# A decode layer on one core: PV in four column tiles, one loop over all batches, and w3 and w4 laid out in long runs

## The chip, the core and the metric

The kernel runs on one core of a Trainium2 chip. A core has five engines that run their own instruction streams and meet at semaphores: TensorE (PE, matrix products, with weight loads shown apart as PEld), VectorE (DVE), ScalarE (ACT), GpSimd (POOL) and SyncE (SP). Sixteen DMA engines bring data from the memory of the chip (HBM) into the core's SBUF. Products land in PSUM. The metric is the device time of one execution in microseconds (us): before the change the median of nine runs is 193.39 us, from 193.25 to 193.49.

## What is computed

One decode step of a transformer layer for 8 batches with one token each: attention over the last 2048 positions of a cache, and then an MLP. The mixer shifts tokens in time, and with one token its branch is zero, so w1 and w2 are never read.

```python
B, Sq, D = 8, 1, 512
Hq, Hkv, Sk, Dh = 32, 8, 8192, 128          # W = 2048, rep = 4
x = A_x
# A: attention
q = layernorm(x) @ wq                       # B, 32 heads, 128
scores = einsum("bhqd,bhkd->bhqk", q, k) * Dh ** -0.5
p = softmax(scores)
o = einsum("bhqk,bhkd->bhqd", p, v)
h = x + o.reshape(B, Sq, Hq * Dh) @ wo      # wo 4096 x 512
# B: MLP on layernorm(h); hs = 0
x1 = layernorm(h)
h2 = gelu(layernorm(x1) @ w3) @ w4          # w3 512 x 1792, w4 1792 x 512
out = h + x1 + h2
```

All arrays are bf16. The two caches give 64 MB of reads, wq and wo 4 MB each, w3 and w4 1.75 MB each.

## The kernel before

**Tiles.** K and V of one batch and four of the eight KV heads form one tile of 2 MB: partition = position block times head, and 64 positions of 128 numbers (16 KB in one run) in each partition. Sixteen K tiles and sixteen V tiles are numbered `t = 2*batch + gq`. The array `slots` has `NS = 10` places of that size. `place` (L234 to L243) says which tile goes where, and `order` (L228 to L233) in what order SP issues the loads. SP issues every load from HBM but that of x, on one queue, in the order of `order`; `free_slot` (L253) makes SP wait first where a place still holds something that is read. A wait on SP holds up all loads behind it. The last two slots hold wq first, then wo.

**Work of a K tile.** `pe_T` (L456) transposes a quarter of a tile (16 matmuls of 128x128, L473) into one of two PSUM buffers, ACT copies one half out (`act_Elo`, L496), DVE the other (`dve_Ehi`, L500). `pe_QK` (L502) multiplies the transposed keys of four KV heads with their queries, one KV head in each of four column tiles of 32 (L516). A batch has eight such quarters.

**Softmax.** When the eight scores are done, DVE takes the maximum (`dve_max`, L521), ACT the exponential (`act_exp`, L539), PE transposes the probabilities (`pe_P`, L480), and DVE multiplies them with a mask while it copies them out (`dve_pT`, L572) so that each head's weights are zero at other heads' positions. `pe_LB` (L556) spreads the sums of the softmax over the rows.

**PV.** `pe_PV` (L581) takes one V tile in 16 matmuls: 64 columns of weights from `pT_sb`, four blocks of values (512 columns) streaming past, two column tiles (L595). The result in PSUM holds four partial blocks side by side of which each row needs one. DVE picks and adds them in four instructions with weights that hold the reciprocal of the sum (`dve_O1`, L602 to L613), PE adds partitions (`pe_oT`, L620) and DVE copies to `o_all` (`dve_oT`, L626). At the end `pe_place` (L649) turns `o_all` into the layout `opl` that the output projection reads.

**Order on PE.** `pe_block` (L663) is written out by hand: block `i` has K quarters of batch `i`, the softmax transposes of batch `i-1` and PV of batch `i-2`. Block 0 stands ahead of the loop, blocks 1 to 7 are a hardware loop (L706), and what is left of PV of the last two batches comes behind it (L751 and following). `need` (L448) is PE's wait: it subtracts what it waited for, so that the loop body can be the same each time.

**Tail.** `pe_proj` (L789, L796) does o @ wo in 128 matmuls with wo as weights, `pe_stats` and `dve_norms` the two layernorms, `pe_h3` (L857) the product with w3, ACT the gelu, `pe_fin` (L878, L887) the residual and the product with w4 in four column tiles; each waits for the pieces of its weights: wo in four cuts, w3 in two halves, w4 in three cuts (`W4_CUT`). DVE (L898), ACT (L907) and SP (L294) write the result. For w3, each partition reads rows of 3584 bytes (L285); for w4, pairs of rows, 2048 bytes (L287).

Of the kernel before, what the change touches and what calls it, by code (L numbers as in the profile page):

```python
# [6 lines left out]
dt = mybir.dt  # L7
# [4 lines left out]
B = 8  # L12
# [19 lines left out]
NS = 10  # L32
# [4 lines left out]
def bass_sequential_preLN__sliding_block_cached__mixer_s_mlp__decode_kernel(  # L37
# [24 lines left out]
    with es:  # L62
# [30 lines left out]
        P_sb = sb([128, CC * 128], dt.bfloat16, "P_sb")  # L93
        pT_sb = sb([128, 2, CC, 64], dt.bfloat16, "pT_sb")
        maskT = sb([128, CC // 2 * GL, 32], dt.bfloat16, "maskT")
        sel = sb([128, GL], dt.float32, "sel")
        headc = sb([128, NT * R], dt.float32, "headc")
        lspread = sb([128, 128], dt.float32, "lspread")
        par_sel = sb([128, 2, GL * R], dt.float32, "par_sel")
        hsel = sb([128, GL * R], dt.float32, "hsel")  # L100
        gq_of = sb([128, 2], dt.float32, "gq_of")
        qi_of = sb([128, NT], dt.float32, "qi_of")
        mrl = sb([128, 2, 2, NT], dt.float32, "mrl")
        o_sum = sb([128, 2, DH], dt.float32, "o_sum")
        mtile = sb([128, 3, 32], dt.float32, "mtile")
        mrow = sb([128, 3, 32], dt.float32, "mrow")
        lcol = sb([128, 2, 2], dt.float32, "lcol")
        lsum = sb([128, 1], dt.float32, "lsum")
        lsel = sb([128, 2], dt.float32, "lsel")
        rL = sb([128, 2, 2], dt.float32, "rL")  # L110
        iota_f = sb([128, 128], dt.float32, "iota_f")
        selp = sb([GL * R, NT, 4 * GL * R], dt.bfloat16, "selp")
        o_all = sb([GL * R, 2, B, DH], dt.bfloat16, "o_all")
# [28 lines left out]
        pv_ps = [misc, b6]  # L142
        LB = S_ps[:, 1, 0:2]
        OT = slice(0, DH)
        H3 = slice(384, 384 + FC * B)

        sem_slot = [S(f"sem_slot{i}") for i in range(NS)]
# [20 lines left out]
        sem_lsel = S("sem_lsel")  # L168
        sem_LB = S("sem_LB")
        sem_qc = S("sem_qc")  # L170
        sem_PV = S("sem_PV")
        sem_O1 = S("sem_O1")
        sem_oTm = S("sem_oTm")
        sem_oT = S("sem_oT")
        sem_oTA = S("sem_oTA")
        sem_pl = S("sem_pl")
# [31 lines left out]
        POOL_ZERO = 3  # L208

        def pool_prog(e):  # L210
# [10 lines left out]
            e.memset(selp[:], 0.0).then_inc(sem_pool, 1)  # L221
# [6 lines left out]
        early = NTILE - 2  # L228
        order = [("k", t) for t in range(4)] + [("v", 0), ("v", 1), ("k", 4), ("v", early), ("k", 5)]
        for t in range(2, NTILE - 4):  # L230
            order += [("v", t), ("k", t + 4)]
# [3 lines left out]
        for t in range(NTILE):  # L235
            place["k", t] = 4 + t if t < 2 else t % 2
            place["v", t] = 4 + t - (NTILE - 4) if t >= NTILE - 4 else 2 + t % 2
# [719 lines left out]
```

## Time and profile before

The profile shows one execution. Its device time was 193.19 us; the span from its first to its last instruction is 191.4 us, so 1.79 us lie around the span.

| what | value |
|---|---|
| median of nine runs | 193.39 us (193.25 to 193.49) |
| profiled execution, device time | 193.19 us |
| its span | 191.4 us |
| PE busy | 147.3 us, 77% of the span |
| PE weight loads busy | 101.2 us |
| DVE busy | 105.2 us |
| ACT busy | 90.3 us |
| read from HBM | 79.18 MB |
| mean granted TensorE clock | 0.948 |

Busy times of engines overlap. An engine that is busy for 77% of the span need not be what sets its end: idle time on it says only that it waited for something. What ended last is told by the chain of waits, followed back from the last instruction.

### The profile page before, as it was taken

How to read it: one execution, taken by the hardware profiler on the slowest of the kernel's cores; microseconds unless marked ns; L12 is line 12 of the kernel's file. 1: busy time of each engine (PE TensorE's matmuls, PEld its weight loads, DVE VectorE, ACT ScalarE, POOL GpSimd, SP SyncE). 2: the span in 40 equal slices, each digit the busy share in tenths (PEclk: the TensorE clock that was granted, in tenths of full speed). 3: DMA queues.
4: the chain of work that ended last, by engine and by line, in shares of the span. 5: the costliest groups of instructions: out<-in, count | busy, mean ns of one | idle time of the engine just before them, and what ended most of it. 6: DMA issues, size and time to landing. Idle time of an engine off the chain costs nothing. (4 is left out here: it accounts for less than half of the span.)

```text
span 191.4 us, 4850 instructions
## 1 busy us (share of the span) xinstructions
PE 147.3 (77%) x2028; PEld 101.2 (53%) x2028; DVE 105.2 (55%) x287; ACT 90.3 (47%) x113; POOL 1.9 (1%) x14
## 2 busy tenths in 40 slices
PE   2027998796999769886988688959996888777854
PEld 0003976582956455645564547456755465343742
DVE  6401757474458474747474747547666657585141
ACT  3301676862746275526553564447344835406041
POOL 4000000000000000000000000000000000000000
PEclk9999999999699999999999999978999999999655
DMA  6999999999999999999999999999999999999991
GB/s 228 431 431 435 431 428 418 423 435 431 438 421 431 435 425 431 435 435 435 423 431 435 425 431 433 431 438 421 435 435 425 428 431 438 435 425 403 417 401 55
DMA packets 6857, 79.31 MB, mean 414 GB/s; under 512 B 688, under 2 KB 704, under 8 KB 2368
## 3 DMA queue, kind: packets, MB, share of 16 engines
q1 hardware_dynamic: 6832, 79.18, 97.4%
q8 instruction: 6, 0.10, 0.2%
q14 instruction: 3, 0.02, 0.0%
q10 hardware_dynamic: 16, 0.01, 0.0%
HBM read 79.18 MB, written 0.01 MB: 414 GB/s over the span
## 5 line engine op out<-in xcount | busy, mean ns | idle before, releaser
L496 ACT ACTIVATE kT_sb<-kT_ps 128x1024 bf16<-128x1024 bf16 x64 | 64.6, 1027 | 67.2 <-PE kT_ps L473 66.8
L473 PE MATMUL kT_ps<-perm_b,slots 128*128 128x128 bf16 x1024 | 70.0, 227 | 21.3 <-PEq L454 21.2
L473 PEld LDWEIGHTS kT_ps<-perm_b,slots 128*128 128x128 bf16 x1024 | 62.6, 102 | 31.7 <-issue 31.7
L500 DVE COPY kT_sb<-kT_ps 128x1024 bf16<-128x1024 bf16 x64 | 43.2, 688 | 26.8 <-PE kT_ps L473 26.8
L516 PE MATMUL S_ps<-kT_sb,qcur 128*32 128x512 bf16 x256 | 22.5, 387 | 0.7 <-PEq L454 0.7
L546 ACT ACTIVATE P_sb<-S_ps,mtile 128x1024 bf16<-128x1024 f32 x16 | 17.8, 1115 | 2.5 <-DVE mtile L537 2.4
L595 PE MATMUL b<-slots,pT_sb 128*64 128x512 bf16 x128 | 16.5, 384 | 1.3 <-PEq L454 1.3
L577 DVE TENSOR_TENSOR pT_sb<-kT_ps,maskT 128x1024 bf16<-128x1024 bf16 x16 | 10.5, 686 | 10.7 <-PE kT_ps L489 10.7
L595 PE MATMUL misc<-slots,pT_sb 128*64 128x512 bf16 x128 | 15.3, 382 | 0.8 <-PEq L454 0.8
L526 DVE TENSOR_REDUCE mtile<-S_ps 128x1 f32<-128x512 f32 x8 | 5.5, 692 | 13.5 <-PE S_ps L516 13.5
L595 PEld LDWEIGHTS misc<-slots,pT_sb 128*64 128x64 bf16 x128 | 6.8, 109 | 8.5 <-issue 3.8
L595 PEld LDWEIGHTS b<-slots,pT_sb 128*64 128x64 bf16 x128 | 6.2, 109 | 9.2 <-issue 5.7
L516 PEld LDWEIGHTS S_ps<-kT_sb,qcur 128*32 128x32 bf16 x256 | 5.3, 94 | 8.3 <-issue 4.1
L489 PEld LDWEIGHTS kT_ps<-ident_b,P_sb 128*128 128x128 bf16 x128 | 7.2, 98 | 4.1 <-issue 4.1
L489 PE MATMUL kT_ps<-ident_b,P_sb 128*128 128x128 bf16 x128 | 8.7, 220 | 0.6 <-PEq L454 0.6
L611 DVE SCALAR_TENSOR_TENSOR o_sum<-b,mrl,o_sum 128x128 f32<-128x128 f32 x24 | 8.4, 351 | 0.8
L611 DVE SCALAR_TENSOR_TENSOR o_sum<-misc,mrl,o_sum 128x128 f32<-128x128 f32 x24 | 8.4, 351 | 0.8
L395 PE MATMUL S_ps<-slots,xlnT 128*8 128x512 bf16 x32 | 3.6, 626 | 5.8 <-DMA slots<-in_A_wq_dram 5.8
L412 DVE TENSOR_SCALAR q_sb<-S_ps 128x512 bf16<-128x512 f32 x1 | 0.7, 691 | 9.2 <-PE S_ps L395 9.2
L626 DVE CAST o_all<-misc 16x128 bf16<-16x128 f32 x7 | 1.9, 279 | 6.5 <-PE misc L620 6.4
L395 PEld LDWEIGHTS S_ps<-slots,xlnT 128*8 128x8 bf16 x32 | 1.0, 117 | 7.5 <-issue 7.5
L657 ACT ACTIVATE opl<-kT_ps 128x224 bf16<-128x224 f32 x1 | 1.2, 1176 | 6.7 <-PE kT_ps L649 6.7
(104 smaller groups left out, 82.5 us busy)
## 6 DMA issues: line engine op xcount, KB each, us to landing
slots<-in_A_k_cache_dram SPq DMA_DIRECT2D x16, 2048.0 KB, 14.2
slots<-in_A_v_cache_dram SPq DMA_DIRECT2D x16, 2048.0 KB, 16.6
slots<-in_A_wq_dram SPq DMA_DIRECT2D x1, 4096.0 KB, 12.4
slots<-in_A_wo_dram SPq DMA_DIRECT2D x1, 2048.0 KB, 30.7
slots<-in_B_w_dram SPq DMA_DIRECT2D x2, 896.0 KB, 32.0
slots<-in_A_wo_dram SPq DMA_DIRECT2D x1, 1024.0 KB, 32.5
slots<-in_A_wo_dram SPq DMA_DIRECT2D x2, 512.0 KB, 33.7
slots<-in_B_w_dram SPq DMA_DIRECT2D x1, 1024.0 KB, 25.7
```

The source lines that it names most:

```text
L395: ins = e.matmul(S_ps[32 * j:32 * j + B, k, :], xlnT[:, kc * B:(kc + 1) * B], wq_v[:, kc, n0:n0 + 512], start=(kc == 0), stop=(kc == KC - ...
L473: ins = e.matmul(kT_ps[t % 2][:, c * 128:(c + 1) * 128], src[:, c * 128:(c + 1) * 128], perm_b[:, :], is_transpose=True)
L489: ins = e.matmul(kT_ps[half][:, c * 128:(c + 1) * 128], P_sb[:, half * W // 2 + c * 128:half * W // 2 + (c + 1) * 128], ident_b[:, :], is_ ...
L496: e.activation(kT_sb[:, i % NKT, 0:W // 2], kT_ps[i % 2][:, 0:W // 2], ACT.Copy).then_inc(sem_Elo, 1)
L500: e.tensor_copy(kT_sb[:, i % NKT, W // 2:W], kT_ps[i % 2][:, W // 2:W]).then_inc(sem_Ehi, 1)
L516: ins = e.matmul(S_ps[32 * gl:32 * (gl + 1), 0, :], qcur[:, GL * gq + gl, o:o + 32], kv[:, gl, :, :], start=(t == 0), stop=(t == 2 * NT - ...
L526: ins = e.tensor_reduce(mtile[:, 2, 0:1], S_ps[:, 0, :], AX.X, ALU.max)
L546: e.activation(P_sb[:, half * W // 2:(half + 1) * W // 2].rearrange("r (k g) -> r k g", g=GL), s_rep, ACT.Exp, bias=mtile[:, j, 0:1], scal ...
L577: e.tensor_tensor(pT_sb[:, :, half * hc:(half + 1) * hc, :].rearrange("p a c (g x) -> p (c g) a x", g=GL), kT_ps[half][:, 0:W // 2].rearra ...
L595: ins = e.matmul(pv_ps[gq][64 * a:64 * (a + 1), :].rearrange("p (q d) -> p q d", d=DH), pT_sb[:, gq, cc, :], vq[:, cc, :, :], start=(cc < ...
L611: ins = e.scalar_tensor_tensor(o_sum[:, gq, :], pv_ps[gq][:, q * DH:(q + 1) * DH], w[:, q:q + 1], o_sum[:, gq, :], ALU.mult, ALU.add)
L626: e.tensor_copy(o_all[:, gq, b, :], pv_ps[gq][0:GL * R, OT]).then_inc(sem_oT, 1)
```

## The change

Five things change together.

1. **PV.** `pe_PV` takes a V tile in 64 matmuls of 32 weight columns with 128 columns streaming, in four column tiles: column tile `q` takes quarter `q` of the positions, and both V tiles of a batch add into the same 128x128 result. To choose 16 of the 32 columns, `pT_sb` has strips of 48 with zeros in the middle. The result holds one block for each row, so `dve_O1` is one instruction, and `pe_OP` (four fp32 matmuls with `selw`, which also adds up the quarters) writes the projection's layout; `act_OP` copies it to `opl`. `pe_oT`, `dve_oT`, `o_all`, `pe_place` and their copies go.
2. **Loop.** All eight blocks are in the loop. Block `i` does the transposed softmax of batch `i-1` behind its first four K quarters, and PV of batch `i-1` behind its last score. In block 0 the softmax part runs on zeros, and PV is skipped. PV of the last batch comes behind the loop.
3. **Places and order.** K has slots 0 and 1, V 2 and 3, the last batch's V 4 and 5, w3 slot 6. K tiles 2 and 3 now wait for the transposes of tiles 0 and 1. A V load waits for PV of the batch before.
4. **w3 and w4.** A partition takes 4 neighbouring rows of w3 and 14 of w4, so each load has one run of bytes per partition: 7168 for a half of w3, and 8192, 4096 and 2048 for the cuts of w4. To fit, the model dimension is numbered `p*4 + k`, and the weights of `pe_proj` are read with a stride of 4 elements, those of `pe_h3` with a stride of 14, the streamed w4 in `pe_fin` and the output with a stride of 4.
5. **Setup.** Other constant tiles on DVE, and POOL clears `selw`, `P_sb` and `pT_sb`.

```diff
-NS = 10
+NS = 9
...
+        order = [("k", 0), ("k", 1), ("vl", 0), ("k", 2), ("v", 0), ("k", 3), ("v", 1)]
+        for b in range(1, NB - 1):
+            order += [("k", 2 * b + 2), ("k", 2 * b + 3), ("v", 2 * b), ("v", 2 * b + 1)]
+        order += [("vl", 1), ("wo", 0), ("wo", 1), ("w3", 0), ("w4", 0)]
+        place = {("vl", 0): 4, ("vl", 1): 5, ("w3", 0): 6, ("w4", 0): 0, ("wo", 0): NS - 2, ("wo", 1): NS - 1}
...
+                    if kind == "k" and b:
+                        e.wait_ge(sem_Thi, NT * (t - 1))
+                    if kind == "v" and b:
+                        e.wait_ge(sem_PV[gq], b)
...
-                                    B_w3.rearrange("(k p) f -> p k f", k=KC)[:, k0:k1, :]).then_inc(sem_w3[i], 16)
+                                    B_w3.rearrange("(p k) f -> p k f", k=KC)[:, k0:k1, :]).then_inc(sem_w3[i], 16)
...
-                    w4_rows = B_w4.rearrange("(c p j) n -> p c (j n)", p=128, j=2)
+                    e.wait_ge(sem_Thi, NT * (NTILE - 1))
+                    w4_rows = B_w4.rearrange("(p c) n -> p (c n)", c=FC)
...
+        def pe_LB(e):
+            if e is not None:
+                for half in range(2):
+                    ins = e.matmul(LB, lspread[:, :, :].rearrange("p q h -> p (q h)"), lsum[:, half:half + 1],
+                                   start=(half == 0), stop=(half == 1))
+                ins.then_inc(sem_LB, 1)
...
+        def pe_PV(e, slot, gq, cs=range(CT)):
+            for c in cs:
+                for q in range(NT):
+                    k = q * CT + c
+                    ins = e.matmul(pv_ps[32 * q:32 * (q + 1), :], pT_sb[:, c, q, 16 * gq:16 * gq + 32],
+                                   slots[:, slot, k * DH:(k + 1) * DH], start=(gq == 0 and c == 0),
+                                   stop=(gq == 1 and c == CT - 1), tile_position=(0, 32 * q), skip_group_check=True)
+            if c == CT - 1:
+                ins.then_inc(sem_PV[gq], 1)
+
+        def dve_O1(e, b):
+            e.wait_ge(dve_self, cnt["dve_self"])
+            e.wait_ge(sem_PV[1], b + 1)
+            e.tensor_scalar(o_sum[:, :], pv_ps, rL[:, :], None, ALU.mult).then_inc(sem_O1, 1)
...
+            for q in range(4):
+                ins = e.matmul(op_ps(b), selw[:, q, :], o_sum[:, NJ * q:NJ * (q + 1)], start=(q == 0), stop=(q == 3))
+            ins.then_inc(sem_OP, 1)
...
         def pe_block(e, i, later=None):
+            for t in range(NT):
                 pe_T(e, i, t)
+            pe_P(e, i, 0)
+            pe_P(e, i, 1)
+            pe_LB(e)
             pe_QK(e, p)
             pe_QK(e, p + 1)
+            for t in range(NT, 2 * NT):
+                pe_T(e, i, t)
+                pe_QK(e, p + t - 2)
+            pe_QK(e, p + 6)
+            pe_QK(e, p + 7)
+            with nullcontext() if e is None else e.If_ne(later, 0):
+                for gq in range(2):
+                    need(e, sem_v[gq], 16 * i)
+                    if e is not None:
+                        pe_PV(e, 2 + gq, gq)
+                pe_OP(e, i - 1)
...
-                    ins = e.matmul(hT_ps[:, k * B:(k + 1) * B], wo_at(h)[:, k * 128:(k + 1) * 128],
+                    ins = e.matmul(hT_ps[:, k * B:(k + 1) * B], wo_at(h).rearrange("r (p k) -> r k p", k=KC)[:, k, :],
...
-                                       w3_sb[:, kc, c * 256:(c + 1) * 256].rearrange("p (q j) -> p j q", j=2)[:, j, :],
+                                       w3_sb[:, kc, :].rearrange("r (p c) -> r c p", c=FC)[:, fc, :],
...
-                                   w4_sb[:, fc, j * DQ:(j + 1) * DQ], start=False, stop=(fc == FC - 1),
+                                   w4_sb[:, fc, :].rearrange("r (p j) -> r j p", j=NQ)[:, j, :], start=False, stop=(fc == FC - 1),
```

## The prediction

> **What bounds the kernel now.** I read the slices of the span first, then the chain of waits, then a steady stretch on PE.
>
> ```profile
> DMA  6999999999999999999999999999999999999991
> GB/s 228 431 431 435 431 428 418 423 435 431 438 421 431 435 425 431 435 435 435 423 431 435 425 431 433 431 438 421 435 435 425 428 431 438 435 425 403 417 401 55
> q1 hardware_dynamic: 6832, 79.18, 97.4%
> ```
>
> All sixteen DMA engines are full from the second slice to the last but one, and SP's one queue fills 97.4% of the span: 186.5 of 191.4 us. The rate is about 431 GB/s and falls to 403, 417 and 401 only in the three slices that carry the late weights. The chain of waits in order of time:
>
> ```profile
> 166.40 21.54 DMA slots<-in_B_w_dram
> ...
> 187.98 0.60 PE b L887 x16
> 188.58 0.03 issue
> 188.60 0.41 PE b L887 x8
> 189.02 0.02 issue
> 189.04 0.28 DVE xln_b L898
> ```
>
> The end hangs on the last two cuts of w4. By the landing records they are complete at 187.93 and 188.56, and eight matmuls, two copies and the store follow. A steady stretch of the timeline on PE:
>
> ```profile
> 102.20 0.62 PE L516 MATMUL S_ps<-kT_sb,qcur 128*32 128x512 bf16 x8
> 102.75 1.92 PE L595 MATMUL misc<-slots,pT_sb 128*64 128x512 bf16 x16
> 104.59 0.40 PE L516 MATMUL S_ps<-kT_sb,qcur 128*32 128x512 bf16 x4
> ```
>
> PV of a tile takes 1.85 us from start to start, and PE is free at 104.99. The next transposes start only at 106.58, when their K tile has landed (106.44 by the records). PE waits for DMA, once per batch. So a change on PE, ACT or DVE gains nothing unless DMA ends earlier, and costs something only if it starves the queue or makes the tail late.
>
> **DMA: what is removed.** The trace's packet records have one duration per size: 2048 bytes 84 ns, 3584 bytes 140, 4096 bytes 159, 8192 bytes 309. Between the last two of these and 3584, 7168 bytes come to 271 ns. Over 16 engines:
> - before: w3 512 x 140 / 16 = 4.48 us, w4 896 x 84 / 16 = 4.70; together 9.18.
> - after: w3 256 x 271 / 16 = 4.34, w4 128 x (309 + 159 + 84) / 16 = 4.42; together 8.76.
>
> The saving is 0.42 us. The windows show the same slope:
>
> ```profile
> 100.00:140.00 40.00, 34.10 (x443) 23.64 (x440) 24.26 (x65) 20.83 (x25) 0.00 (x0) 0.96 1.01 431
> 179.00:182.50 3.50, 2.99 (x103) 2.90 (x100) 0.38 (x2) 0.00 (x0) 0.00 (x0) 0.50 1.02 413
> 182.50:186.50 4.00, 2.35 (x66) 1.87 (x65) 1.86 (x11) 2.24 (x5) 0.00 (x0) 0.50 1.04 403
> ```
>
> The last number is GB/s: 431 for 16 KB runs, 413 for w3, 403 for w4. [...] All other loads keep their bytes and runs, and the count of loads on the queue is the same.
>
> **The queue: what is moved.** By the landing records the tiles behind wq land every 4.86 us from 18.0 on (from the third on some 1.1 us later, for one engine lags), and a batch of four tiles is 19.45 us. SP is in order, so each wait must end about 1.1 us before the queue runs dry (first issue at 0.73, first data at 1.78). K tiles 2 and 3 were loaded without a wait. K tile 2 now waits for the transposes of tile 0: they start about 18.8 (pe_qT, 1.06 us, comes ahead of them) and end near 24.2, and tile 2's place in the stream opens near 26.6. K tile 3: end of block 0's transposes near 31.6, place at 36.4. K tile 5: near 48.3, place at 50.9; this is the tightest, 1.5 us to spare. In the steady state a V load waits for PV of the batch before, and has 8 us; a K load 6. w4 now waits for the transposes of tile 14 only, near 155, and its place opens at 183. No hole in the queue: cost 0. If a wait ended late, the hole would be as long as the delay beyond these margins.
>
> **PE per block.** From the starts in the timeline:
> - 8 transposed quarters x 0.98 = 7.84; probabilities 1.0; eight scores 2.3.
> - LB: L560 takes 0.2 from start to start for one fp32 matmul; two, 0.45.
> - Waits: the second probability transpose for ACT's copy of quarter 3, 0.45; the last score for quarter 7, 0.5.
> - PV: 128 matmuls. Not in the trace in this form. Nearest is L887, four column tiles, 128 columns streaming: groups of four start 107 ns apart, 27 ns each, at half clock. [...] L887 is the same form but for its 8 weight columns, so 3.4, less than the 3.75 of before.
> - New wait on O1, with only the loop's end and the next quarter behind it: PV's end to DVE 0.2, L608's 0.34, back 0.15. It replaces eight instructions of 0.35 on DVE.
> - OP: eight fp32 passes at 109 ns (spacing of L560), 0.9; loop and branch 0.2.
>
> The sum is 17.7 us; as the second V tile lands 14.6 us after the block's K tile, some 18.3. Below 19.45: DMA still sets the pace, cost 0; without that cover every us over 19.45 counts per block. ACT's 32-column copy (0.27, by L636) and the broadcast mask on DVE (0.69 as L577, even twice that) hide under waits. POOL's clearing of 5120 columns at 1 ns (qcur: 480 in 0.49) ends near 8 us, and is wanted at 23; DVE's setup has 5.5 us until wq lands.
>
> **The tail.** K tile 14 lands at 150.4: block 7's last score ends at 163.0, PV of batch 6 at 166.7 (its V tile lands at 165.0), OP at 168.5. Then probabilities, LB, mask (1.6), PV (last V at 169.9) until 173.4, O1 and OP 1.8, copy 0.4: projection from 175.8, against 177.94 before. Its last cut of wo lands at 179.70, so it ends at 180.3 instead of 181.7. Norms 2.7: 183.0. w3's second half lands near 183.9, h3 ends 184.8, gelu and first weights 0.65. w4's cuts then land at 186.27, 187.50 and 188.13: PE waits for each, and ends at 188.55 instead of 189.01.
>
> Strided weights: L857 with stride 2 starts every 27 ns, L796 with stride 1 as well, L372 with stride 4 every 34 to 37. Stride 14 is in no row. [...] Ends: 27 ns, and 109 (L560's fp32 loads of 128 columns). By the row h3 costs 1.5 us; at 53, double, 3.0, and ends at 186.0, just in time for w4. So up to 53 ns it costs nothing; I take no cost. w4 streams with a stride of 8 bytes, and the output is written with one: only eight of those 56 matmuls and the copies come behind the last landing, so that even a doubling of the matmuls costs 0.2 us there; I take 0[...].
>
> **Sum.** 193.19 - 0.42 = 192.77 for the profiled execution; the median of the runs is 0.20 above it, so 192.97, and I forecast **192.95 us**. No change cannot be told from a change under 0.2%, 0.39 us here: the forecast lies at the edge.
>
> **Rivals.**
> 1. *The slowest DMA engine decides (no change).* The last landing spreads over 1.88 us among the engines, and one load of the chain is complete only with the slowest. At 25.0 us a 16 KB packet of the instruction queue took 0.88 us on one engine, and the spread of the next landing went from 0.82 to 1.78. The new program fetches its instructions at other moments. Against it: six such packets raised the largest lag only once. If the laggard takes a small packet more, the 0.42 is eaten: 193.4; with a whole one, 193.9.
> 2. *Strided weights make the tail late (slower).* Place: h3, between the norms and w4; it decides from 53 ns per weight load. At 109: 183.0 + 6.1 + 0.65 + 1.3 + 0.4 = 191.5 against 189.0: **195.9 us**. If wo's stride is hit too, more. [...] Against: stride 2 and 4 at 27 to 37 ns.
> 3. *PE becomes the bound in the loop (slower).* It decides from 40 ns per PV matmul (block 19.45). At 60 ns the block is 22 us, 2.6 over the batch's DMA time, and seven blocks bring some 18, of which the tail's lead of before takes up 1: about 210 us. For it: twice as many matmuls per tile column, an exposed wait. Against: L887.
>
> **How the numbers follow.** Main case 0.60: 192.5 to 193.3 by itself, three quarters of it faster by more than 0.2%, since the lag of the slowest engine can also shrink. Rival 1: 0.15, mostly within 0.2%. Rival 2: 0.15. Rival 3: 0.10. Faster 0.44 (main) and 0.01 (rival 1); same 0.16 and 0.09; slower 0.05 (rival 1) and 0.25 (rivals 2 and 3). The range takes main, rival 1 and most of rival 2: 192.3 to 196.2; what is left out is the upper part of rival 2, rival 3, and a little below.
>
> **What would show it.** DMA still full in all middle slices; w3 and w4 at 420 GB/s; last w4 landing near 188.1; idle before each block's first transposes near 1 us; PV of a batch 3.4 us or less; projection from about 175.8; L857's successor below 53 ns. The forecast is wrong if DMA slices show holes, if the chain ends in PE's h3 or PV rather than in w4, or if the last landing comes no earlier.

## The result: slower by half a per cent, and the profile after

| | before | after |
|---|---|---|
| median, us (executions) | 193.42 (30) | 194.46 (10) |
| lowest to highest, us | 193.16 to 193.78 | 193.72 to 195.06 |
| profiled execution, us | 193.19 | 194.41 |
| its span, us | 191.4 | 192.5 |
| last landing of w4, slowest DMA engine | 188.56 | 189.12 |
| last landing of w4, first DMA engine | 186.68 | 187.39 |

The trace holds sixteen landings for each load, taken here as one for each of the sixteen DMA engines: the earliest is the first engine's, and the load is complete with the latest, the slowest engine's.

The ratio is 1.0054, with a 95% interval of 1.0043 to 1.0065. The forecast was 192.95 us, faster; the change made the kernel 1.04 us slower. The time lies inside the stated range of 192.3 to 196.2 us only because that was drawn wide enough for two rivals; the main case ended at 193.3. All three signs of being wrong that the prediction named came: a hole in the DMA slices, a chain that runs through h3 instead of w4, and a last landing that is no earlier. Two rows of the slices of the span, on the page of the kernel after:

```profile
PEclk9999999696999995899999859999999699999556
...
GB/s 226 429 436 432 426 426 426 422 432 436 378 424 432 432 426 434 436 426 426 426 432 436 432 432 436 432 429 432 436 432 426 422 432 432 436 432 397 427 396 20
```

One slice of 4.8 us, the eleventh (from 48.1 to 52.9 us), moved 378 GB/s where the two beside it moved 436 and 424. The kernel before has no such slice. In the row above, TensorE's granted clock dips in slices 8, 10, 16, 17, 23, 24 and 32, ahead of the dip at the end that the kernel before has too; that one has two more, around slices 11 and 28. Two windows of the kernel after show the hole (the last two numbers are the DMA share and GB/s):

```profile
51.00:52.00 1.00, 1.00 (x60) 0.85 (x64) 0.59 (x1) 0.00 (x0) 0.00 (x0) 1.00 0.99 311
52.00:57.00 5.00, 4.31 (x133) 4.02 (x122) 2.31 (x9) 3.91 (x7) 0.00 (x0) 1.00 0.97 400
```

The queue runs dry and starts again: the engines are idle for 0.23 us on average, and over the five microseconds after that the rate is 400 GB/s, where the kernel before moved 426 in the same window. By the packet records, 13 of the 19 packets of 16 KB that start between 51 and 52 us take 0.83 to 1.08 us where they take 0.61 elsewhere; of the 71 that start in the three microseconds after that, 4 take over 0.8. The load that came late is K tile 5, in the timeline of SP:

```profile
50.08 0.54 SPq L247 DMA_DIRECT2D slots<-in_A_k_cache_dram  x1
```

It waits for T7 of block 1 (T0 to T7 are the eight transposed quarters of a block). The timeline of PE shows why T7 was late (start, duration, then the idle time ahead of it in brackets):

```profile
43.56 1.11 PE L439 MATMUL kT_ps<-perm_b,slots 128*128 128x128 bf16 x16 [1.98 <-PEq L422]
...
45.15 1.89 PE L439 MATMUL kT_ps<-perm_b,slots 128*128 128x128 bf16 x16
...
47.52 1.21 PE L439 MATMUL kT_ps<-perm_b,slots 128*128 128x128 bf16 x16
...
48.98 1.07 PE L439 MATMUL kT_ps<-perm_b,slots 128*128 128x128 bf16 x16
```

These are T4 to T7, 16 transposes each. T4 waits until 43.56 for K tile 3, T5 takes 1.89 us instead of 1.07, and T7 ends at 50.05. The clock records put TensorE at half clock from 44.4 to 47.8 us, behind the idle stretch of 1.98 us. The kernel before had shown the same: two of the idle stretches in its loop, 1.98 us ahead of 48.32 and 1.92 ahead of 126.37, are followed by 3.4 us at half clock each, and none of its shorter ones (up to 1.6 us) is.

The end of the chain of waits after:

```profile
150.00 30.60 DMA slots<-in_A_wo_dram
180.60 0.05 issue
180.65 0.71 PE S_ps L669 x16
...
184.06 3.55 PE misc L729 x56
187.60 0.32 PE b L750 x8
187.92 0.04 issue
187.96 1.84 PE b L759 x51
189.79 0.02 issue
189.82 0.45 ACT xln_b L779
```

w4 is no longer in it: from wo's last cut (180.60; 179.70 before) it runs through PE to the end. h3 (L729) takes 3.55 us for its 56 matmuls, 63 ns each. The rows for the groups of the kernel before, then after:

```profile
L857 PE MATMUL misc<-uT,slots 128*128 128x8 bf16 x56 | 1.7, 168 | 1.5 <-DVE uT L833 1.5
...
L907 ACT ACTIVATE xln_b<-b 8x128 bf16<-8x128 f32 x2 | 0.5, 270 | 2.7 <-PE b L887 2.7
```

```profile
L536 PE MATMUL misc<-slots,pT_sb 128*32 128x128 bf16 x1024 | 16.3, 219 | 1.9 <-PEq L422 1.9
...
L729 PE MATMUL misc<-uT,slots 128*128 128x8 bf16 x56 | 3.5, 202 | 1.5 <-DVE uT L706 1.5
...
L779 ACT ACTIVATE xln_b<-b 8x128 bf16<-8x128 f32 x2 | 0.9, 446 | 1.9 <-PE b L759 1.9
```

The busy time, ahead of the comma, doubled for h3 (1.7 to 3.5 us) and nearly for the output copies (0.5 to 0.9). PV (L536) is cheap: 16.3 us for eight batches.

In the profiled execution, the 1.1 us by which the span grew can be split like this: the last landing 0.56 later; the final matmuls end 0.65 instead of 0.45 us behind it, for h3 holds them up, 0.20; from there to the store 0.99 instead of 0.64, the strided copies, 0.35. In sum 1.11. This is bookkeeping; what causes each part is for the experiments.

### The profile page after: what moved, and what is told of

It reads as the page before. It is cut to its first block, busy times and chain, and to the rows that moved or that the text cites. A ratio compares the mean times of both kernels' runs of the same rounds, so it can differ in the third digit from the quotient of the medians.

```text
span 192.5 us, 6348 instructions
## 1 busy us (share of the span) xinstructions
PE 146.8 (76%) x2848; PEld 118.9 (62%) x2848; DVE 86.2 (45%) x183; ACT 92.9 (48%) x119; POOL 6.4 (3%) x17
## 5 line engine op out<-in xcount | busy, mean ns | idle before, releaser
L461 ACT ACTIVATE kT_sb<-kT_ps 128x1024 bf16<-128x1024 bf16 x64 | 64.4, 1023 | 48.3 <-PE kT_ps L439 48.1
L504 ACT ACTIVATE P_sb<-S_ps,mtile 128x1024 bf16<-128x1024 f32 x16 | 17.7, 1109 | 19.4 <-DVE mtile L499 19.4
L536 PE MATMUL misc<-slots,pT_sb 128*32 128x128 bf16 x1024 | 16.3, 219 | 1.9 <-PEq L422 1.9
L536 PEld LDWEIGHTS misc<-slots,pT_sb 128*32 128x32 bf16 x1024 | 14.7, 97 | 3.4 <-issue 3.3
L526 DVE TENSOR_TENSOR pT_sb<-kT_ps,mask 128x1024 bf16<-128x1024 bf16 x18 | 12.4, 690 | 3.5 <-PE kT_ps L455 3.4
L455 PE MATMUL kT_ps<-perm_p,P_sb 128*128 128x128 bf16 x144 | 10.9, 219 | 3.0 <-PEq L422 2.9
L455 PEld LDWEIGHTS kT_ps<-perm_p,P_sb 128*128 128x128 bf16 x144 | 8.4, 97 | 5.2 <-issue 5.0
L555 PE MATMUL b<-o_sum,selw 128*128 128x32 f32 x56 | 7.8, 285 | 4.3 <-PEq L422 4.3
L555 PEld LDWEIGHTS b<-o_sum,selw 128*128 128x128 f32 x56 | 7.2, 202 | 5.3 <-issue 5.3
L669 PE MATMUL S_ps<-opl,slots 128*128 128x8 bf16 x128 | 5.0, 175 | 1.9 <-DMA slots<-in_A_wo_dram 1.3
L287 DVE TENSOR_SCALAR ident_f<-iota_f 128x128 f32<-128x128 f32 x1 | 5.7, 5682 | 1.3 <-POOL iota_f L207 1.3
L288 DVE TENSOR_SCALAR ident_b<-iota_f 128x128 bf16<-128x128 f32 x1 | 5.6, 5606 | 0.0
```

The source lines that it names most:

```text
L287: e.tensor_single_scalar(ident_f[:], iota_f[:], 0.0, ALU.is_equal)
L288: ins = e.tensor_single_scalar(ident_b[:], iota_f[:], 0.0, ALU.is_equal)
L455: ins = e.matmul(kT_ps[half][:, c * 128:(c + 1) * 128], P_sb[:, k * 128:(k + 1) * 128], perm_p[:, :], is_transpose=True)
L461: e.activation(kT_sb[:, i % NKT, 0:W // 2], kT_ps[i % 2][:, 0:W // 2], ACT.Copy).then_inc(sem_Elo, 1)
L504: e.activation(P_sb[:, half * W // 2:(half + 1) * W // 2].rearrange("r (k g) -> r k g", g=GL), bass.AP(tensor=S_ps[:, :, :].tensor, offset ...
L526: e.tensor_tensor(bass.AP(tensor=pT_sb[:, :, :, :].tensor, offset=h0 * NT * 48, ap=[[CT * NT * 48, 128], [48, CT // 2 * NT], [32, 2], [1, ...
```

## The experiments

All times are medians, with the ratio to the kernel before run beside them (193.35 to 193.48 us in the six sets). The ratio takes in all executions and not the median alone, so a few long ones raise it. There is one profile per kernel, and where the executions spread it need not be a typical one. The theory at the start had three causes: the hole near 51 us, the stride of 14 in h3, the strided output copies. The rivals were the hole alone, the layouts alone, and some cost of the new loop itself.

### The layouts

**e3** puts all the new layouts into the kernel before and keeps its loop. Besides these two lines, x, w4's stream and the output get the stride of 4, and w4 its long runs:

```diff
-  ... wo_at(h)[:, k * 128:(k + 1) * 128]
+  ... wo_at(h).rearrange("r (p k) -> r k p", k=KC)[:, k, :]
-  ... w3_sb[:, kc, c * 256:(c + 1) * 256].rearrange("p (q j) -> p j q", j=2)[:, j, :]
+  ... w3_sb[:, kc, :].rearrange("r (p c) -> r c p", c=FC)[:, fc, :]
```

> The kernel before with the new layouts alone (wo stride 4, w3 stride 14, w4 in long runs, strided output). Its projection starts at 178, two us later than in the changed kernel, so every strided load is on the path. Theory of three causes: last landing near 188.2, projection 0.7 us longer, h3 3.5 us, end of PE near 191.1, copies 0.9: 195.5 to 196.0 us. If the layout alone made the loss of 1 us: 194.4. If strides cost nothing and only the hole does: 193.0.

Measured: 195.66 us, ratio 1.0118 [1.0104, 1.0133]. The chain of waits of e3 at its end:

```profile
185.40 3.53 PE misc L855 x56
188.94 0.31 PE b L876 x6
189.25 0.04 issue
189.29 1.89 PE b L885 x53
191.18 0.02 issue
191.20 0.45 ACT xln_b L905
```

w4 had landed at 188.57, as before (188.56), but the projection (L795) took 4.4 us at a stride of 4, h3 started at 185.40, and the final matmuls began at 189.29, when all of w4 had long been there. The layouts by themselves make the old kernel 2.3 us slower.

**e7** and **e8** take the two halves of it. The new numbering of the hidden dimension (f) changes h3's weights (stride 14) and w4's rows; that of the model dimension (d) changes wo's and x's weights, w3's runs (7168 bytes), w4's stream and the output.

```diff
e7, in the kernel before:
-  w4_rows = B_w4.rearrange("(c p j) n -> p c (j n)", p=128, j=2)
+  w4_rows = B_w4.rearrange("(p c) n -> p (c n)", c=FC)
e8, in the kernel before:
-  B_w3.rearrange("(k p) f -> p k f", k=KC)
+  B_w3.rearrange("(p k) f -> p k f", k=KC)
-  e.activation(out_sb[:, j * DQ:(j + 1) * DQ], ...
+  e.activation(out_sb[:, :].rearrange("b (p j) -> b j p", j=NQ)[:, j, :], ...
```

> The kernel before with only the numbering of the hidden dimension of w3 and w4 new: w4 in long runs, the weights of h3 at a stride of 14 columns. If the price of the stride decides: h3 takes 3.5 us instead of 1.7 and ends after the last cut of w4 has landed, so about +1.6 us against w4's landing (which comes 0.2 earlier), less the 0.3 us by which the final matmuls ran ahead: 194.6 to 195.0 us. If weight loads at stride 14 cost nothing beside the stride of 4: 193.2 us.

> The kernel before with only the numbering of the model dimension new: wo read at a stride of 4 columns as weights, w3 in runs of 7168 bytes, w4 streamed at a stride of 4, the output copied at a stride of 4. If the output copies decide: +0.35 us for them, and up to 0.7 us of the longer projection that w4's landing hides: 193.7 to 194.1 us. If the w4 stream at a stride of 4 costs time: over 194.3 us, the final matmuls longer than 32 ns each. If none of it costs: 193.2 us.

Measured: e7 194.14 us, ratio 1.0038 [1.0025, 1.0051]; e8 193.81, ratio 1.0019 [1.0010, 1.0028]. e7 costs less than expected, a miss: its h3 took 3.54 us from 184.40 and ended at 187.94, ahead of w4's last cut (188.50), and the final matmuls ended at 189.99, 1.0 us later than before (189.01). e8 is a hit: the 56 final matmuls took 1.80 us; with contiguous columns they took 1.66 in e7 and 1.81 in e12 below, so no cost of a stream at a stride of 4 can be told. The copies took 0.9 instead of 0.6 us. The halves cost 0.75 and 0.42 us, both together 2.29: a late projection is hidden by w4 as long as h3 is short, and a long h3 as long as the projection is early.

**e2** is the opposite, the new loop with all layouts of before.

> The changed kernel with the layouts of before for wo, w3, w4 and the output (unit stride, w3 stride 2, runs of 3584 and 2048 bytes); new PV, loop and order stay. Theory of three causes: h3 1.7 us, copies 0.57 us, the hole near 51 us stays, last landing 189.4: 194.0 to 194.3 us. If the layout alone is the loss: 193.4 or less. If the hole alone is: 194.8, for the long runs are lost as well.

Measured: 194.39 us, ratio 1.0054 [1.0041, 1.0067], just above the 194.0 to 194.3 us of the theory of three causes and short of the 194.8 of the hole alone. h3 and the copies are back, and the time stays: now w4's landing ends the chain, at 189.16 instead of 188.56.

```profile
166.46 22.08 DMA slots<-in_B_w_dram
...
189.21 0.41 PE b L761 x8
189.62 0.02 issue
189.65 0.28 DVE xln_b L772
```

So the new loop costs 1.0 us by itself, and in the profiled execution (193.89 us, 0.70 above that of the kernel before) 0.60 of it is the later landing. In this profile K tile 5 was issued at 48.84, with T4 to T7 at full clock, and its landing cost the slowest engine nothing; where the 0.60 comes from is taken up below. **e12** puts back the d half alone, and so the contiguous output.

> The changed kernel with the old numbering of the model dimension (wo read in contiguous columns, w3 in runs of 3584 bytes, w4 streamed and the output copied in contiguous columns), and the new numbering of the hidden dimension kept (h3 at stride 14, w4 in long runs). The output copies go back from 0.90 to 0.55 us, w3 lands 0.1 us later; h3 stays at 3.5 us. If the output copies' term is real and nothing hides it: 194.1 to 194.3 us. If the tail is bound by w4's landing alone: 194.5 us.

Measured: 194.03 us, ratio 1.0034 [1.0021, 1.0047]: 0.43 us less than the change, and the copies of ScalarE 0.5 us (L779) instead of 0.9. The copies account for 0.35 of it, so the term is real.

### Moving the load, first try

**e1** gives K tile 5 more time by putting a load that needs no slot of the loop ahead of it; **e4** is the same with the layouts of before.

```diff
-  order += [("k", 2 * b + 2), ("k", 2 * b + 3), ("v", 2 * b), ("v", 2 * b + 1)]
+  order += [("k", 2 * b + 2)] + [("vl", 1)] * (b == 1) + [("k", 2 * b + 3), ...]
```

> The changed kernel with one load moved: the last V tile, which waits for nothing, goes between K tile 4 and K tile 5 in SP's order, so that K tile 5 has 4.9 us more before the queue runs dry. Theory of three causes (a hole in the DMA queue near 51 us; weight loads with stride 14 in h3; strided output copies): no slice below 420 GB/s between 20 and 170 us, last landing of w4 between 188.1 and 188.6 instead of 189.12, but h3 still takes 3.5 us and now ends last, so only half of it is won: 193.7 to 194.0 us. If the hole alone is the loss: 193.0. If the layout alone is: 194.4, unchanged.

> Both: last V early, and the layouts of before. What is left of the change is PV in four column tiles, the loop over all batches and the order. Theory of three causes: DMA full, last landing 188.5, PE ends near 189.0: 193.3 to 193.5 us, the time of before. If the new PV or loop costs something itself: over 193.7. If it gains something at the end: under 193.1.

Measured: e1 198.05 us, ratio 1.0272 [1.0237, 1.0308]; e4 194.66, ratio 1.0057 [1.0044, 1.0070]. Both are misses, for a reason that I had not weighed. The GB/s of e1:

```profile
GB/s 222 441 428 428 425 408 421 425 435 431 435 430 431 435 431 436 428 431 428 431 428 428 431 431 435 428 435 435 428 435 435 435 428 431 431 405 422 414 88 2
```

The hole near 51 us is gone, but now DMA has finished two slices ahead of the end. A tile put ahead of K tile 5 moves all later K tiles by 4.86 us, the last one too, and the last block, the projection and the norms are late: h3 starts at 187.58 in e1 instead of 184.06, and ends after w4 has landed (189.06). In e4 the short h3 ends ahead of that landing, so it loses far less. What stands where at the end of the queue is as much a part of an order as where it waits.

### Keeping TensorE's clock up

**e5** and **e6** fill TensorE's idle time ahead of T0 and T4 with matmuls into columns that nothing reads; e6 has the layouts of before and more clearing matmuls at the start.

```diff
+  def pe_fill(e, n):
+      for _ in range(n if e is not None else 0):
+          e.matmul(misc[:, 256:384], perm_b[:, :], perm_b[:, :], start=True, stop=True, ...)
+  pe_fill(e, 40)        # ahead of T0 and ahead of T4
```

> The changed kernel with 40 matmuls of 128x128 into unused columns ahead of T0 and ahead of T4 in every block, where TensorE otherwise sits idle for about 2 us; the order of all loads is unchanged. If the hole in the queue near 51 us comes from TensorE's half clock (44.4 to 47.9 us), T7 of block 1 ends about 1.2 us earlier, K tile 5 is issued near 48.8 us instead of 50.08, no packet of 16 KB is slow there, and the last landing comes 0.6 to 0.8 us earlier, while h3 (3.55 us) and the output copies (0.90 us) stay as they are: 193.6 to 193.9 us. If the hole has another cause (T7 late for its K tile and not for the clock): 194.4 us, with K tile 5 issued near 50 us still. If the added matmuls make the blocks late: over 195 us.

> The changed kernel with the layouts of before for wo, w3, w4 and the output, with the 40 added matmuls ahead of T0 and T4 in every block, and with 20 instead of 2 clearing matmuls at the start[...]. If holes in the queue are all that is left of the loss once the layouts are back: 193.3 to 193.6 us, the time of before, with landings of the K tiles 4.86 us apart on the first engine. If what is left is the lag of the slowest DMA engine: 194.2 to 194.4 us, as without the added matmuls, with a lag of over 2 us at the last load.

Measured: 210.09 us, ratio 1.0871 [1.0829, 1.0913], and 209.19, ratio 1.0835 [1.0813, 1.0858]: the third outcome that e5 named. In the timeline of e5:

```profile
61.91 2.40 PE L564 MATMUL misc<-perm_b 128*128 128x128 bf16 x40
64.15 3.93 PE L439 MATMUL kT_ps<-perm_b,slots 128*128 128x128 bf16 x64
...
70.47 2.41 PE L564 MATMUL misc<-perm_b 128*128 128x128 bf16 x40
...
82.43 0.78 PE L564 MATMUL misc<-perm_b 128*128 128x128 bf16 x11
```

Forty of them take 2.24 us, and a block takes 82.43 - 61.91 = 20.52 us, more than the 19.45 of its four tiles. PE sets the pace, and the queue has a hole in every block (328 GB/s from 58 to 62 us and from 78 to 82, where it moves 422 to 434 in between). It says nothing of the clock, but it measures the block: without the 4.5 us of filling, 16.0 us are left for PE.

**e9** (and **e10**, with the layouts of before) is a smaller dose at one place: twelve such matmuls, ahead of T4 alone.

> The changed kernel with 12 matmuls of 128x128 into unused columns ahead of T4 in every block (0.67 us at full clock), where TensorE waits for the second K tile: a smaller dose than the 40 and 40 before, and only at the place that decides the hole near 51 us. If the half clock after the idle stretch at 41.6 us is what makes T7 of block 1 late: T4 to T7 run at full clock, K tile 5 is issued near 48.8 to 49.2 us, the last landing comes 0.5 to 0.8 us earlier, and the time is 193.7 to 194.0 us. If 0.67 us of work cannot keep the clock up: K tile 5 is issued at 50 us or later, 194.4 to 194.7 us. If a delay of 0.67 us in each block opens holes later: a step of over 0.2 us in the landings of the later K tiles, and over 195 us.

> The changed kernel with the layouts of before for wo, w3, w4 and the output, and with the same 12 matmuls ahead of T4. If holes in the queue are what the new loop costs: 193.4 to 193.8 us. If the lag of the slowest DMA engine is: 194.2 to 194.5 us as without the matmuls, with a lag of over 2.1 us at the last load.

Measured: e9 194.55 us, ratio 1.0057 [1.0041, 1.0074]; e10 194.80, ratio 1.0083 [1.0050, 1.0116]. In e9 T4 to T7 ran at full clock and K tile 5 was issued at 48.84 instead of 50.08, and the time did not follow. That the twelve matmuls kept the clock up is not shown: TensorE still stood idle for 1.92 us between them and T4, and in e2, without them, K tile 5 was issued at 48.84 too. The first engine's last landing came 0.50 us earlier (186.89). But the slowest engine's came at 189.31, later than after the change (189.12): its step over K tile 5 was 0.90 us too long. DMA's idle time up to 52 us fell from 0.23 to 0.06 us, yet until 53.5 us only some fifteen of the sixteen engines were at work at a time. A load is complete when the slowest engine is, and this restart cost the first engine 0.30 us and that one 0.90. In the profile of e10 K tiles 2 and 5 were issued late (leads of 3.38 and 1.74 us), but these cost the slowest engine only 0.06 and nothing; its last landing at 190.06 comes from other steps, 1.31 us of it while wo was loaded.

### Moving the load, second try

**e13** loads K tile 3 ahead of V tile 0. **e14** cuts V tile 0 into two halves, one on each side of K tile 3, which gives that tile 2.4 us and leaves every later load in its place. **e15** is e14 with the layouts of before, **e16** with the d half put back as in e12.

```diff
-  order = [("k", 0), ("k", 1), ("vl", 0), ("k", 2), ("v", 0), ("k", 3), ("v", 1)]
e13:
+  order = [("k", 0), ("k", 1), ("vl", 0), ("k", 2), ("k", 3), ("v", 0), ("v", 1)]
e14, e15, e16:
+  order = [("k", 0), ("k", 1), ("vl", 0), ("k", 2), ("va", 0), ("k", 3), ("vb", 0), ("v", 1)]
```

> The changed kernel with K tile 3 loaded right behind K tile 2, ahead of V tile 0 instead of behind it. K tile 3 then lands 4.86 us earlier, T7 of block 1 no longer waits for it, and K tile 5 is issued near 47 us; but K tile 3 itself now waits for T7 of block 0 (29.8 us) with its place at 31.9. If a wait must end some 2.5 us ahead of its place: no hole near 51, a smaller one (0.2 to 0.6 us) near 32, and 194.0 to 194.4 us. If a lead of 2 us is enough: no hole at all, and 193.6 to 194.0. If the hole does not matter for the slowest engine: 194.4 to 194.6.

> The changed kernel with V tile 0 loaded in two halves (8 KB packets), one on each side of K tile 3, so that K tile 3 lands 2.4 us earlier with a lead of 4 us. T7 of block 1 then ends near 47.6 us and K tile 5 is issued 3.3 us ahead of its place: no hole at all. If the restart is what the new loop costs the slowest engine: last landing 188.3 to 188.6 us (189.12 before this edit), and with h3 and the output copies left as they are 193.7 to 194.0 us. If the fetches near 174 us decide: last landing still near 189, and 194.3 to 194.6 us.

> The same split of V tile 0, with the layouts of before for wo, w3, w4 and the output. If restarts in the queue are all that the new loop costs: the time of before, 193.2 to 193.6 us. If the fetches of instructions that hit the slowest engine near 174 us are: 194.1 to 194.4 us, with a lag of over 2 us at the last load.

> The same split of V tile 0, with the old numbering of the model dimension and the new one of the hidden dimension (w4 in long runs, h3 at stride 14): the candidate for the fastest. If restarts are the loss: 193.2 to 193.5 us, about the time of before, since w4's long runs save 0.2 us and h3 gives 0.2 back. If the fetches are: 193.9 to 194.1 us, as without the split.

| kernel | median, us | ratio | 95% interval |
|---|---|---|---|
| e13 | 194.89 | 1.0082 | 1.0065 to 1.0098 |
| e14 | 193.89 | 1.0035 | 1.0023 to 1.0048 |
| e15 | 193.53 | 1.0025 | 1.0009 to 1.0040 |
| e16 | 193.33 | 1.0006 | 0.9995 to 1.0017 |

The slices of e14:

```profile
PEclk9999999699969999999699979999999699999556
...
GB/s 220 437 431 431 427 420 417 434 434 437 431 425 434 424 431 432 431 434 437 427 431 434 424 431 434 431 434 437 427 431 434 424 431 434 431 434 400 422 398 28
```

and its PE in block 1, T4 to T7 again:

```profile
41.67 1.07 PE L446 MATMUL kT_ps<-perm_b,slots 128*128 128x128 bf16 x16
...
43.00 1.07 PE L446 MATMUL kT_ps<-perm_b,slots 128*128 128x128 bf16 x16
...
44.33 1.07 PE L446 MATMUL kT_ps<-perm_b,slots 128*128 128x128 bf16 x16
...
45.66 1.07 PE L446 MATMUL kT_ps<-perm_b,slots 128*128 128x128 bf16 x16
```

From the second slice to the 36th none is below 417 GB/s. T4 follows the scores with no idle time, all four quarters run at full clock, T7 ends at 46.73 instead of 50.05, and the last landing is at 188.44. The medians of e14, e15 and e16 lie where the restart theory put them. Not all else does: e15 and e16 still landed w4 late, at 188.90 and 189.06, e15 with the lag of over 2 us (2.03) that its expectation had named as the sign of the other theory, and e15's ratio stays above 1. In e13 the hole has moved, not gone, and costs more than expected:

```profile
GB/s 219 434 434 434 428 421 329 417 431 431 428 426 434 434 431 433 424 428 431 434 434 428 431 431 434 431 431 434 428 431 434 434 431 431 424 431 400 425 396 24
```

So moving this one load takes most of the new loop's loss out of the median. It is worth 0.57 us with the new layouts (194.46 to 193.89), 0.86 with those of before (194.39 to 193.53), and 0.70 with the d half back (194.03 to 193.33). With the load moved, the d half costs 0.56 (193.89 to 193.33). By the intervals, each of these is good to some 0.3 us. With both gone no loss can be measured: e16, which has the new PV, the new loop and w4 in long runs, cannot be told from the kernel before. It is the fastest that I found; none beats the kernel before by more than can be measured.

Not all of this is the hole. The profiles show two things that held the slowest engine back: the waits with little lead, and a step while the four cuts of wo are loaded.

| profile | slowest engine: extra at late waits, us | lag behind the first engine gained over wo, us | last V tile landed | w4 landed |
|---|---|---|---|---|
| before | none | 0.0 | 169.89 | 188.56 |
| after | 0.56 (K tile 5) | 0.57 | 170.22 | 189.12 |
| e2 | 0.0 (K tiles 2, 5) | 0.69 | 169.96 | 189.16 |
| e12 | 0.59 (K tile 5) | 0.56 | 170.41 | 189.40 |
| e14 | none | 0.28 | 169.81 | 188.44 |
| e15 | none | 0.68 | 169.67 | 188.90 |
| e16 | 0.20 (K tile 2) | 0.25 | 170.00 | 189.06 |

Up to the last V tile the move brings the slowest engine forward by 0.41 us from after to e14 and by 0.41 from e12 to e16, which fits the hole. From e2 to e15 it is 0.29, but these two differ already at K tile 1 (24.10 and 23.77 us), ahead of every moved load: the profile of e2 is its fastest of five executions, and what its slower ones lose is not on record. The step at wo is in 13 of the 16 profiles with the new loop, 0.25 to 1.56 us, and in none of the four with the old one. Rival 1 of the prediction had named such a thing. A 16 KB packet of the instruction queue comes ahead of it (at 174.20 us in the kernel after), but the four with the old loop have one near there too (172.6 to 175.2 us) without a step. So the cause of the step stays open, and so does its share in the gain of the medians.

The profiles of these runs show how much lead a wait needs. Lead is the time from SP's issue of a load to the moment when the first engine has done the packets ahead of it; the extra time is what the landing of that load took beyond the 4.86 us of a tile:

| run, K tile | lead, us | extra, first engine | extra, slowest engine |
|---|---|---|---|
| e14, 5 | 4.65 | 0.01 | -0.01 |
| after, 2 | 4.63 | 0.01 | 0.00 |
| e16, 2 | 3.44 | 0.45 | 0.20 |
| e9, 15 | 3.44 | -0.02 | 0.00 |
| e18, 3 | 3.25 | 0.00 | 0.00 |
| e13, 2 | 3.19 | 0.17 | 0.15 |
| e17, 13 | 3.02 | -0.02 | 0.00 |
| e2, 5 | 2.77 | 0.10 | 0.00 |
| e17, 5 | 2.66 | 0.68 | 1.29 |
| e9, 5 | 2.50 | 0.30 | 0.90 |
| e10, 5 | 1.74 | 0.19 | -0.01 |
| after, 5 | 1.22 | 0.86 | 0.56 |
| e11, 5 | 1.00 | 1.10 | 0.00 |
| e13, 3 | 0.77 | 1.24 | 1.33 |

The table is a choice; over all runs it is this. From 3.6 us on no wait cost the first engine more than 0.10 us. Of 18 waits with a lead of 2.5 to 3.5, ten cost it 0.16 to 0.68 and eight no more than 0.10; what tells them apart is open. With a lead under 1.3 us every one of 19 cost it what was missing to a lead of 2.0 to 2.2 us. The slowest engine scatters, from nothing to 1.8 us at leads of about 1.

### The spread of the executions

In 22 executions each, e15 lay between 193.20 and 195.41 us and e16 between 193.08 and 194.73, where the kernel before stays within 193.12 and 193.77: seven executions of e15 and three of e16 lie above 194.2. In the profile of e16 block 0 had run at a slower pace until about 21 us (12 matmuls in the microsecond from 19 us, where e14 had 21), T3 ended at 23.44, and K tile 2 had the short lead of the table. **e17** gave K tile 2 more lead with a quarter of V tile 0 ahead of it; **e18** starts TensorE's work earlier.

```diff
e17:
+  order = [..., ("vl", 0), ("va", 0), ("k", 2), ("va", 1), ("k", 3), ("va", 2), ("va", 3), ("v", 1)]
e18, e16 with, ahead of the Q projection:
+  for k in range(4):
+      e.matmul(S_ps[:, k % 2, :], zrow_b[0:1, :], x_sb[0:1, :], start=True, stop=True)
```

> The changed kernel with V tile 0 loaded in four quarters (4 KB packets): one ahead of K tile 2, one ahead of K tile 3, two behind it; old numbering of the model dimension, new one of the hidden dimension. If K tile 2's late wait makes the group of executions near 194.5 us: no such group, all executions 193.0 to 193.5 us, median 193.1 to 193.3, no step of over 0.15 us in the first engine's landings. If the group has another cause: it stays, median 193.3 to 193.5 us.

> The kernel of e16 (V tile 0 in halves around K tile 3, old numbering of the model dimension) with four clearing matmuls of 512 columns repeated ahead of the Q projection, where TensorE waits for wq from 11.3 to 13.0 us. If the group of executions near 194.5 us comes from block 0 at half clock: T0 to T3 of block 0 take 4.0 us in every execution, the group goes, and the executions lie at 193.0 to 193.5 us with a median of 193.1 to 193.3. If it has another cause: about one execution in seven stays above 194 us.

Measured: e17 194.01 us (193.50 to 195.14), ratio 1.0032 [1.0013, 1.0051]; e18 193.39 (193.04 to 194.35), ratio 1.0006 [0.9995, 1.0017]. Both miss. In e17 PE now waits 4.1 us for K tile 2, runs T0 to T3 of block 1 at half clock, and is late for K tile 5 again. In e18 the four matmuls did not make block 0 faster: T0 to T3 of block 0 took 5.35 us in its profile, about as in e16's (5.1; 4.1 in e14's). What sets the pace of block 0 from one execution to the next stays open.

### A side effect in the setup

In the kernel after, VectorE's two identity matrices took 5.68 and 5.61 us, against 0.87 and 0.79 before. **e11** holds GpSimd's large clears until they are done.

```diff
+  e.wait_ge(sem_dveP, DVEP_IDENT)
   e.memset(lsum[:], 0.0)
   e.memset(P_sb[:], 0.0).then_inc(sem_exp, 2)
```

> The changed kernel with GpSimd's clears of lsum, P_sb and pT_sb held until VectorE has made its identity matrices (L287, L288 took 5.7 and 5.6 us each beside those clears, 0.87 and 0.79 in the kernel before). If VectorE is slow there because GpSimd clears at the same time: both take under 1 us again. The time stays at 194.3 to 194.6 us, since xlnT is ready 1.7 us before wq lands either way.

The rows of the kernel after and of e11:

```profile
L287 DVE TENSOR_SCALAR ident_f<-iota_f 128x128 f32<-128x128 f32 x1 | 5.7, 5682 | 1.3 <-POOL iota_f L207 1.3
```

```profile
L288 DVE TENSOR_SCALAR ident_f<-iota_f 128x128 f32<-128x128 f32 x1 | 1.3, 1306 | 1.3 <-POOL iota_f L207 1.3
```

5.68 us became 1.31, not under 1; smaller clears (qcur 0.49 us, selw 0.52) were not held back. The time stayed, 194.33 us, ratio 1.0071 [1.0042, 1.0100], as expected of work that ends before wq lands.

## Why the prediction was wrong

Two steps failed, and each alone is enough to turn the sign. With the load moved and the new layouts kept (e14) the kernel is still slower, 193.89 us; with the hole kept and the d half back (e12) it is too, 194.03. With both gone (e16) it is as fast as before, 193.33, and no faster: of the saving it keeps w4's part, 0.28 of the 0.42 us forecast, and the time does not show it.

**"No hole in the queue: cost 0."** This is the first step. It was put together from two numbers, and both were too kind. T7 of block 1 was put near 48.3; it ended at 50.05. T4 started at 43.56 and four quarters at full clock take 5.06 us (e14, 41.67 to 46.73), which would have been 48.6; the rest, 1.4 us, is the half clock behind the idle stretch. I had costed every transposed quarter at 0.98 us, from a stretch in which PE is idle for 1.6 us at most and the clock is full, and had priced neither the longer idle time of the new loop nor the two half-clock pieces in the trace of before. And the margin of 1.1 us was that of the very first load on empty engines. The form of the estimate was right, a hole as long as what the margin lacks, but behind a full queue the margin was 2.0 to 2.2 us in 19 waits: K tile 5, with a lead of 1.22, cost the first engine 0.86 and the slowest 0.56. At 48.3 us the lead would have been 2.6 to 3; there waits cost between nothing and 0.7. The loss of the new loop in the medians, 0.57 to 0.86 us, has the step at wo in it besides, whose cause is open.

**"Up to 53 ns it costs nothing; I take no cost."** Measured 63 ns per matmul of h3. I took the rows of strides 2 and 4, 27 to 37 ns, though stride 14 had no row; that it might cost more was an estimate, shown by no trace of before. Stride 4 was not free either, 4.4 us for 128 matmuls of wo in e8 against 3.6 in e7 with contiguous columns. Rival 2 named this place; at 63 ns it is worth far less than its 195.9 us: 0.75 in e7, 0.20 of the change by the sum above, and in e16, where the projection is early, nothing that can be measured.

**"The output is written with one ... I take 0."** This is the second step. Measured 0.35 us from the final matmuls to the store, all of it on the path. The two copies of each engine went from 0.28 to 0.45 us each. This was a term with a known place, behind everything, and no row; a bound was owed there and I set it to nothing.

**The saving of 0.42 us** was right in kind. Packets of 7168 bytes took 272 ns (271 forecast), and w3 and w4 together 8.52 us on the slowest engine instead of 8.86: 0.34. In e3, with the old loop, the first engine ended 0.26 us earlier and the slowest where it was. Of rival 1 that much is true: the slowest engine decides, the first engine's gain does not always reach it, and the new loop has a step of its own on that engine, 0.57 us at wo in the profile after. Which engine a fetch of instructions falls on cannot be read from the trace, and no run separates it.

**PE** was costed too dear and safely so: PV 1.97 us per batch, 15 ns per matmul, against 3.4 forecast; the block 16.0 us against 17.7 to 18.3. Rival 3 is out. PE's longest idle stretches in the loop grew, to 2.65, 2.10 and 2.09 us from 1.98 and 1.92, and in the profile after half clock for 3.4 us followed one of 1.98 in the one block whose loads had no lead to spare. How long the stretch is does not decide by itself: e9 kept the full clock behind 1.92 us, and e8 behind 3.04.

**The tail** was late from its start: wo's last cut landed at 180.60, the projection ended at 181.36 (180.3 forecast), the norms took the 2.7 us forecast, and h3 ended at 187.61 instead of 184.8.

## What to carry to other kernels

When an order of loads is changed, work out for every load with a wait the lead between its issue and its place, at the pace that the engine before it has after an idle stretch (T4 to T7 took 6.49 us after, 5.06 in e14), and leave some 4 us (here no wait with a lead of 3.6 us or more cost the first engine over 0.10 us); then look at what the new order does to the last loads. A layout that makes transfers longer is paid by whoever reads with the stride (h3 here 63 ns per matmul instead of 30): price each such reader by a row with that stride, and the readers behind the last landing first. Read the slowest engine's landings beside the first one's (K tile 5 of e9: 0.90 us late on the slowest, 0.30 on the first). Two changes that each hide behind the same transfer do not add: measured alone they cost 0.75 and 0.42 us here, together 2.29.

## What the runs showed of the hardware

- Weight loads of 128 columns at a stride of 14 (28 bytes): 63 ns per matmul for h3, against 30 (1.7 us for 56) at a stride of 2; at a stride of 4, 34 ns (4.4 us for 128) against 28 contiguous. A moving operand at a stride of 4 showed no cost (1.80 us for 56; contiguous 1.66 in e7, 1.81 in e12).
- Copies of 8x128 from PSUM to a bfloat16 output at a stride of 4: 0.45 us on ScalarE and 0.43 on VectorE, against 0.27 and 0.28.
- In the loop of the kernel before TensorE fell to half clock for 3.4 us behind its idle stretches of 1.98 and 1.92 us and behind none of 1.6 us or less. Length alone does not decide: e9 kept the full clock behind 1.92 us and e8 behind 3.04.
- A tile issued less than 1.3 us ahead of its place in the queue, or after the queue had run dry, took 6.9 to 7.1 us from its issue to its landing on the first engine, 2.0 to 2.2 us more than a tile takes in a full queue (4.86; 19 waits).
- In the microsecond from 51 us, in which the engines were idle for 0.23 us on average, 13 of the 19 packets of 16 KB that started took 0.83 to 1.08 us instead of 0.61; over the five microseconds from 52 us the rate was 400 GB/s, where the kernel before moved 426.
- VectorE's compare of 128x128 took 5.68 us beside GpSimd's clears of two bfloat16 tiles (1.79 and 2.65 us), and 1.31 with those held back.
